# Gated mix of two attentions: first loads in tiles of later work, first maxima by four, projections in two PSUM banks, and a rule by segment for the runs of P @ V

## The chip, the cores and the metric

The kernel runs on one core of one Trainium2 chip. The time is the device time of one execution in microseconds (us). Engines are named as in the profile: PE is TensorE (PEld its weight loads), DVE is VectorE, ACT is ScalarE, POOL is GpSimd, SP is SyncE, which issues most of the DMAs from one queue in the order of the program.

## The reference, cut to what matters

Input x has 2048 tokens of 512 values. Two attentions over x with 32 heads of 16 are mixed by a gate per token.

```python
g = sigmoid((x * gate_w).sum(-1, keepdims=True))
# A: full softmax attention
q, k, v = split(x @ wqkv)                       # 32 heads of 16
a = (softmax(q @ k.T / 4) @ v) @ wo
# B: four segments of 512 tokens, causal inside, with a running memory
for s in range(4):
    p = softmax(qs @ ks.T / 4 + mask)           # within the segment
    a_dot = p @ vs
    a_mem = (phi(qs) @ M) / (phi(qs) @ z + 1e-6)    # phi(t) = t + 1 for t > 0, else exp(t)
    o = sigmoid(beta) * a_mem + (1 - sigmoid(beta)) * a_dot
    M += phi(ks).T @ vs;  z += phi(ks).sum(0)
b = concat(o) @ b_wo
out = g * a + (1 - g) * b
```

## The kernel before, in words

**The head.** The weights and x are split into two parts each (a high part, rounded by ScalarE, and the rest, subtracted by VectorE), and each projection is the sum of three products over four blocks of 128: 12 matmuls of 512 columns into one PSUM bank. Such a group is a *slot* (`slot`, L304). There are 96: for each of four chunks of 512 tokens, four tiles of q, four of k and four of v, first for side A (slots 0 to 47), then for side B (48 to 95, in the order q, v, k). A slot has four *places*, one after each three matmuls; what is posted to a place (`post`, `post_at`) is issued there. So the order on every engine is written out by hand.

After the slot of a q or k tile, `qk_tile` (L343) posts its exit to the next slot: at place 0 ScalarE casts the bank to q1 (L352) and SyncE stores it; at place 1 VectorE subtracts q1 from the bank (q2, L359) and SyncE stores that. For side B, phi needs a minimum (L356), an exponential (L363) and one more VectorE pass (L368), all from the bank. q1 and q2 have two buffers each, the bank pool `pr_ps` three. `mem_k` and `mem_q` do the memory's products.

The weights come through `halves` (L319): two loads of 512 KB into a pool `raws` of three buffers, and four splits posted to slots. The first wq half and the first x chunk take all three buffers; the second wq half (L414), wk and wv follow in the same pool on SyncE's queue.

**Maxima.** Each softmax needs its row maximum before the scores are computed again transposed. `max_part` (L207) does one of 2368 such products (L204) into a bank, and VectorE reduces it (L219). The products of successive parts use different rows of the array. `maxs` gives the order; the maxima run `LEAD` = 96 steps ahead of the scores. The first 96 belong to the head: `some_max` (L514) does two at place 1 and two at place 3 of each slot from slot 72 on (24 after the start of side B), in three banks (`me_sm`).

**The steps.** 2368 steps follow, 74 for each pair of units (a unit is four heads and one segment of 512 queries; 64 steps for A, 10 for B). Each step: one score product (`score_part`, L614) into one of three banks, its exponential on ScalarE (L637), one maximum product into one of four banks. Finished pieces of P @ V wait in `queue`. Every third step (`BURST`) `some_values` (L649) takes up to `MOST` = 3 pieces from it, one more where the queue holds over 6, and one more over 13 (L833); successive pieces of one block of keys form one *run*, a single matmul for each head of up to 512 columns (L670). When a unit of side A after the first segment is done, four bursts go to the output product of an earlier segment instead (`shared`, L747), and pieces of P @ V pile up meanwhile. `first["A", 0, 1]` is step 592, where the second segment of side A begins; the third and fourth begin at 1184 and 1776.

Of the kernel before, what the change touches and what calls it, by code (L numbers as in the profile page):

```python
# [10 lines left out]
F32 = mybir.dt.float32  # L11
# [36 lines left out]
def gated_mix(ctx, tc, x, xT, wqkv, a_wo, b_wq, b_wk, b_wv, b_wo, beta, gate_w, out):  # L48
# [229 lines left out]
    with ExitStack() as p0:  # L278
# [7 lines left out]
        pr_ps = p0.enter_context(tc.tile_pool(name="pr_ps", bufs=3, space=PSUM))  # L286
        me_ps = p0.enter_context(tc.tile_pool(name="me_ps", bufs=2, space=PSUM))
        me_sm = p0.enter_context(tc.tile_pool(name="me_sm", bufs=3, space=PSUM))

        ones = wk1.tile([2, CH], F32, name="ones")  # L290
# [28 lines left out]
        def halves(pool, tag, src, load_slot, split_slot):  # L319

            hold = {}

            def load(i):
                hold["raw", i] = raws.tile([128, 2, D], F32, tag="raw", name="raw")
                nc.sync.dma_start(hold["raw", i], src[256 * i:256 * i + 256].rearrange("(k p) d -> p k d", p=128))

            def split(k):
                if k == 0:
                    hold[0] = pool.tile([128, KT, D], F32R, tag=tag + "h", name=tag + "h")
                    hold[1] = pool.tile([128, KT, D], F32R, tag=tag + "l", name=tag + "l")  # L330
                w = hold["raw", k // 2][:, k % 2]
                nc.scalar.copy(hold[0][:, k], w)
                nc.vector.tensor_sub(hold[1][:, k], w, hold[0][:, k].bitcast(F32))
            post_at(load_slot, 2, lambda: load(0))
            post_at(load_slot, 3, lambda: load(1))
            for k in range(KT):
                post_at(split_slot + k // 2, 2 * (k % 2), lambda k=k: split(k))
            return hold
# [4 lines left out]
        def qk_tile(side, w, xc, o, dst, then=None):  # L343

            ps = pr_ps.tile([128, CH], F32, tag="pr", name="pr")
            slot(ps, lambda a, k: w[a][:, k, o * 128:(o + 1) * 128], lambda b, k: xc[b][:, k, :])
            q1 = wk.tile([128, CH], F32R, tag="q1", name="q1")
            q2 = wk.tile([128, CH], F32R, tag="q2", name="q2")
            ph = {}

            def e0():
                nc.scalar.copy(q1, ps)  # L352
                nc.sync.dma_start(dst[0:16].rearrange("d h t -> (d h) t"), raw(q1))
                if then:
                    ph["mn"] = wk1.tile([128, CH], F32, tag="mn", name="mn")
                    nc.vector.tensor_scalar_min(ph["mn"], ps, 0.0)  # L356

            def e1():
                nc.vector.tensor_sub(q2, ps, q1.bitcast(F32))  # L359
                nc.sync.dma_start(dst[16:32].rearrange("d h t -> (d h) t"), raw(q2))  # L360
                if then:
                    ph["ex"] = wk1.tile([128, CH], F32, tag="ex", name="ex")
                    nc.scalar.activation(ph["ex"], ph["mn"], AF.Exp)  # L363

            def e2():
                if then:
                    ph["ph"] = wk.tile([128, CH], F32, tag="ph", name="ph", bufs=4)
                    nc.vector.scalar_tensor_tensor(ph["ph"], ps, 0.0, ph["ex"], op0=ALU.max, op1=ALU.add)  # L368
                    then(ph["ph"])
            for place, f in enumerate((e0, e1, e2)):  # L370
                post(0, place, f)
# [142 lines left out]
        def some_max(place):  # L514
# [6 lines left out]
            run_todo(m + 1)  # L521
            mnext[0] += 2
            run_late(me_ps, "me", mnext[0])
# [286 lines left out]

    filled = [0]
    n = 0
    while n < nS or queue or beside or filled[0] < len(fill):
# [73 lines left out]
```

## Time and profile before

| | us |
|---|---|
| median of 3 runs (1923.2 to 2658.01) | 1924.52 |
| the profiled execution | 1924.45 |
| its span, first to last instruction | 1922.7 |
| busy: PE / DVE / ACT / POOL | 1878.9 / 1612.1 / 1467.3 / 281.4 |
| first exponential of the steps | about 345 |

The span is the profiled execution without what lies before its first and after its last instruction. A matmul that has been issued and waits in line counts as busy, so TensorE's share is not its load; the other engines' shares are. Stages are read in windows of the same execution.

### The profile page before, as it was taken

Reading aid. Unit: us, or ns where it says so; the run is one execution under the profiler, and the core shown is the slowest. Engines: PE = TensorE matmul, PEld = TensorE weight load, DVE = VectorE, ACT = ScalarE, POOL = GpSimd, SP = SyncE. Lnnn points to the kernel's source line nnn. Section 1 sums busy time; section 2 is a strip of 40 time slices with the busy share of each in tenths; the row PEclk is TensorE's granted clock in tenths of the full one; section 3 lists DMA queues with packets and bytes.
Section 4 is the critical chain, followed back from the end, with each engine's and each line's share of the span. In section 5 each row is a group of like instructions: output and inputs, shape, how many; then the busy total and the mean of one; then the engine's idle time right before and its main releaser. Section 6 shows DMA issues by size and latency. Waiting matters only on the chain.

```text
span 1922.7 us, 46247 instructions
## 1 busy us (share of the span) xinstructions
PE 1878.9 (98%) x18081; PEld 1007.5 (52%) x18081; DVE 1612.1 (84%) x2768; ACT 1467.3 (76%) x2864; POOL 281.4 (15%) x497
## 2 busy tenths in 40 slices
PE   7999999999999999999999999999999999999996
PEld 6888766444444444445445445445444454554554
DVE  4235687899999999999999999999999999999810
ACT  3234332788888888888888888888888888888873
POOL 3000000211111111111112111112111111111210
PEclk9999999899999999999999999999999999999999
DMA  6567645334233324343334343334343334343311
GB/s 206 205 226 259 204 156 167 115 99 129 86 107 92 103 87 110 101 108 102 110 97 111 99 107 102 109 99 111 100 110 100 111 101 113 100 111 99 82 54 41
DMA packets 124362, 227.32 MB, mean 118 GB/s; under 512 B 35144, under 2 KB 50152, under 8 KB 123632
## 3 DMA queue, kind: packets, MB, share of 16 engines
q1 hardware_dynamic: 122560, 223.24, 39.5%
q8 instruction: 144, 2.36, 0.5%
q0 software_dynamic: 1296, 0.59, 0.2%
q14 instruction: 74, 0.61, 0.1%
q10 hardware_dynamic: 288, 0.52, 0.1%
HBM read 155.52 MB, written 67.52 MB: 116 GB/s over the span
## 4 chain that ended last, share of the span: by engine, by line
PE 91%; DMA 3%; ACT 3%; DVE 2%; issue 1%; SPq 0%; ACTq 0%; DVEq 0%
PE ops L670 30%; PE st L614 28%; PE sm L204 13%; PE pr L311 11%; PE ops L747 5%; ACT p L637 2%; PE sm L747 1%; DMA qdA<-q 1%; PE num L468 1%; ACT dg L230 1%; DMA kdB<-q 1%; PE mt_ps L194 1%; DVE pm L219 1%; PE mps L499 0%; DMA qdB<-q 0%
## 5 line engine op out<-in xcount | busy, mean ns | idle before, releaser
L637 ACT ACTIVATE p<-st 128x512 f32<-128x512 f32 x2304 | 1217.6, 606 | 190.6 <-PE sm L204 145.1
L219 DVE TENSOR_REDUCE pm<-sm 128x1 f32<-128x512 f32 x2048 | 1285.6, 681 | 79.0 <-PE sm L204 58.6
L204 PE MATMUL sm<-kA,qA 48*128 48x512 f32 x2048 | 752.0, 448 | 0.3 <-DVE pm L219 0.3
L614 PE MATMUL st<-qA,kA 50*128 50x512 f32 x2048 | 702.8, 440 | 7.2 <-ACT p L637 6.5
L670 PE MATMUL ops<-p,vA 128*17 128x512 f32 (+3 forms) x5784 | 558.9, 473 | 0.0
L614 PEld LDWEIGHTS st<-qA,kA 50*128 50x128 f32 x2048 | 335.4, 186 | 400.6 <-ACT p L637 330.2
L204 PEld LDWEIGHTS sm<-kA,qA 48*128 48x128 f32 x2048 | 338.3, 185 | 26.6 <-DVE pm L219 13.4
L670 PEld LDWEIGHTS ops<-p,vA 128*17 128x17 f32 x5784 | 107.5, 95 | 196.7 <-issue 177.4
L204 PE MATMUL sm<-kB,qB 48*128 48x128 f32 (+2 forms) x896 | 170.6, 294 | 0.0
L204 PEld LDWEIGHTS sm<-kB,qB 48*128 48x128 f32 x896 | 136.4, 189 | 8.4 <-DVE pm L219 0.9
L231 POOL TENSOR_SCALAR_AFFINE_SELECT dg<-dg 128x512 f32<-128x512 f32 x128 | 81.2, 637 | 291.7 <-ACT dg L230 291.7
L614 PE MATMUL st<-qB,kB 50*128 50x384 f32 (+3 forms) x512 | 120.3, 342 | 2.9 <-ACT p L637 2.4
L359 DVE TENSOR_TENSOR q<-pr,q 128x512 fp32r<-128x512 f32 x64 | 43.9, 687 | 89.4 <-ACT q L352 80.2
L187 POOL CAST ms<-nm 128x16 fp32r<-128x16 f32 x64 | 12.6, 197 | 724.9 <-DVE nm L180 496.1
L352 ACT CAST q<-pr 128x512 fp32r<-128x512 f32 x64 | 37.4, 585 | 97.6 <-PE pr L311 64.1
L614 PEld LDWEIGHTS st<-qB,kB 50*128 50x128 f32 x512 | 72.1, 185 | 72.7 <-ACT p L637 60.2
L618 POOL TENSOR_SCALAR_AFFINE_SELECT p<-p 128x512 f32<-128x512 f32 x128 | 78.6, 634 | 92.2 <-ACT p L637 91.5
L240 DVE TENSOR_REDUCE pmB<-sm 128x4 f32<-128x512 f32 x128 | 87.1, 681 | 1.4 <-PE sm L204 1.0
L234 DVE TENSOR_REDUCE pmB<-dg 128x4 f32<-128x512 f32 x128 | 86.6, 677 | 0.4 <-POOL dg L231 0.4
L670 PE MATMUL ops<-p,vB 128*17 128x128 f32 (+3 forms) x1224 | 84.1, 394 | 1.5 <-issue 1.5
L230 ACT COPY dg<-sm 128x512 f32<-128x512 f32 x128 | 76.9, 601 | 1.6 <-PE sm L204 1.0
L721 DVE RECIPROCAL rec<-rec 128x32 f32<-128x32 f32 x44 | 15.1, 342 | 71.5 <-DMA rec<-odA 37.3
(128 smaller groups left out, 1553.3 us busy)
## 6 DMA issues: line engine op xcount, KB each, us to landing
kA<-kdA SPq DMA_DIRECT2D x256, 128.0 KB
vA<-vdA SPq DMA_DIRECT2D x32, 544.0 KB
kA<-kdA SPq DMA_DIRECT2D x256, 64.0 KB
qdA<-q SPq DMA_DIRECT2D x32, 256.0 KB
kdA<-q SPq DMA_DIRECT2D x32, 256.0 KB
qdB<-q SPq DMA_DIRECT2D x32, 256.0 KB
qA<-qdA SPq DMA_DIRECT2D x64, 128.0 KB
kdB<-q SPq DMA_DIRECT2D x32, 256.0 KB
```

Source lines behind the costliest of these rows:

```text
L204: nc.tensor.matmul(ps[:, n0:n0 + n], rows(qt[u][:, :, s * 128:(s + 1) * 128], h, 48), rows(k[:, :, k0:k0 + n], h, 48), start=True, stop=True)
L219: nc.vector.tensor_reduce(pm[:, h, s, kc:kc + 1], ps, axis=AX.X, op=ALU.max)
L230: nc.scalar.copy(dg, blocked(ps))
L231: nc.gpsimd.affine_select(out=dg, in_=dg, pattern=[[0, 4], [-1, 128]], base=0, channel_multiplier=1, compare_op=ALU.is_ge, fill=MASKED)
L234: todo.append((m + MASK_T, lambda: nc.vector.tensor_reduce(to, dg.rearrange("p (h s) t -> p h s t", h=2), axis=AX.X, op=ALU.max)))
L240: nc.vector.tensor_reduce(pm[:, 1, h, 3:7], blocked(ps), axis=AX.X, op=ALU.max)
L311: nc.tensor.matmul(ps, l(a, k), r(b, k), start=(n == 0), stop=(n == 11))
L614: nc.tensor.matmul(ps[:, n0:n0 + CH - q0], rows(k[:, :, b * 128:(b + 1) * 128], h, 50), rows(q[:, :, q0:], h, 50), start=True, stop=True)
L618: nc.gpsimd.affine_select(out=x, in_=x, pattern=[[0, 4], [1, 128]], base=0, channel_multiplier=-1, compare_op=ALU.is_ge, fill=0.0)
L637: nc.scalar.activation(p[:, h], ps, AF.Exp, scale=SCALE)
L670: nc.tensor.matmul(ops[32 * h:32 * h + 17, q0:q0 + 128 * w], v[:, 17 * h:17 * h + 17], p[:, h, c0:c0 + 128 * w], start=(i == 0), stop=done ...
L747: nc.tensor.matmul(ps[32 * t:32 * t + 32, 128 * (j % (ps.shape[1] // 128)):128 * (j % (ps.shape[1] // 128)) + 128], held[side, c][:, o, 12 ...
```

## The change

Five things, in the order of the diff:

- TensorE gets ten 128 x 128 products of the identity ahead of all else.
- `pr_ps` has two banks instead of three, `me_sm` four instead of three.
- `halves` can be given tiles to load into. The second wq half and the first half of wk load into the v tile (`early`, not used before slot 8), the rest of wk and half of wv into the tiles of phi (`pairs`, not used before side B). The loads of wq and wk are issued at the start, those of wv at slot 1.
- `qk_tile`: ScalarE copies the bank to `full` first, and everything else reads `full`; the minimum of phi is GpSimd's.
- `some_max` does four maxima at place 3 only, in the slots 14 to 19, 24 to 31 and 36 on from the start of side B (62 to 67, 72 to 79, 84 to 93). `jam` replaces the rule for how many pieces a burst takes.

```diff
-        pr_ps = p0.enter_context(tc.tile_pool(name="pr_ps", bufs=3, space=PSUM))
+        pr_ps = p0.enter_context(tc.tile_pool(name="pr_ps", bufs=2, space=PSUM))
         me_ps = p0.enter_context(tc.tile_pool(name="me_ps", bufs=2, space=PSUM))
-        me_sm = p0.enter_context(tc.tile_pool(name="me_sm", bufs=3, space=PSUM))
+        me_sm = p0.enter_context(tc.tile_pool(name="me_sm", bufs=4, space=PSUM))
+        idle = me_ps.tile([128, CH], F32, tag="me", name="idle")
+        for _ in range(10):
+            nc.tensor.matmul(idle[:, :128], identf, identf, start=True, stop=True)
...
-        def halves(pool, tag, src, load_slot, split_slot):
+        def halves(pool, tag, src, load_slot, split_slot, tiles=None):
             def load(i):
-                hold["raw", i] = raws.tile([128, 2, D], F32, tag="raw", name="raw")
-                nc.sync.dma_start(hold["raw", i], src[256 * i:256 * i + 256].rearrange("(k p) d -> p k d", p=128))
+                t = tiles[i] if tiles else None
+                if t is None:
+                    t = raws.tile([128, 2, D], F32, tag="raw", name="raw")
+                if isinstance(t, list):
+                    for k in range(2):
+                        nc.sync.dma_start(t[k], src[256 * i + 128 * k:256 * i + 128 * k + 128])
+                        hold["raw", 2 * i + k] = t[k]
+                else:
+                    nc.sync.dma_start(t, src[256 * i:256 * i + 256].rearrange("(k p) d -> p k d", p=128))
...
-            post_at(load_slot, 2, lambda: load(0))
-            post_at(load_slot, 3, lambda: load(1))
+            if load_slot is None:
+                load(0)
+                load(1)
+            else:
+                post_at(load_slot, 2, lambda: load(0))
+                post_at(load_slot, 3, lambda: load(1))
...
+            full = wk.tile([128, CH], F32, tag="full", name="full")
             def e0():
-                nc.scalar.copy(q1, ps)
+                nc.scalar.copy(full, ps)
+                nc.scalar.copy(q1, full)
                 nc.sync.dma_start(dst[0:16].rearrange("d h t -> (d h) t"), raw(q1))
                 if then:
-                    nc.vector.tensor_scalar_min(ph["mn"], ps, 0.0)
+                    nc.gpsimd.tensor_scalar_min(ph["mn"], full, 0.0)
             def e1():
-                nc.vector.tensor_sub(q2, ps, q1.bitcast(F32))
+                nc.vector.tensor_sub(q2, full, q1.bitcast(F32))
...
-                    nc.vector.scalar_tensor_tensor(ph["ph"], ps, 0.0, ph["ex"], op0=ALU.max, op1=ALU.add)
+                    nc.vector.scalar_tensor_tensor(ph["ph"], full, 0.0, ph["ex"], op0=ALU.max, op1=ALU.add)
...
+        early = vp.tile([128, NG, 4, 4, 17], F32, tag="vs", name="vs").rearrange("p g b h e -> p (g b h e)")
+        early = [early[:, 1024 * i:1024 * i + 1024] for i in range(2)]
+        wraw.append(early[0].rearrange("p (k d) -> p k d", k=KT))
+        pairs = [[wk.tile([128, CH], F32, tag="ph", name="ph", bufs=4) for _ in range(2)] for _ in range(2)]
...
+        nc.sync.dma_start(wraw[1], wq_src[:, :, 256:512])
...
-        wraw.append(raws.tile([128, KT, 256], F32, tag="raw", name="raw"))
-        nc.sync.dma_start(wraw[1], wq_src[:, :, 256:512])
-        wAk = halves(wp, "wk", wqkv[:, D:2 * D], 0, 2)
-        wAv = halves(wp, "wv", wqkv[:, 2 * D:3 * D], 0, 4)
+        wAk = halves(wp, "wk", wqkv[:, D:2 * D], None, 2, [early[1].rearrange("p (k d) -> p k d", k=2), pairs[0]])
+        wAv = halves(wp, "wv", wqkv[:, 2 * D:3 * D], 1, 4, [pairs[1], None])
...
-            loads(m + 1 + PRE)
-            for i in range(2):
+            loads(m + 3 + PRE)
+            for i in range(4):
...
-        for n in range(24, 64):
-            for place in (1, 3):
-                posted.setdefault((s0 + n, place), []).append(lambda: some_max(0))
+        for n in range(14, 64):
+            if n // 12 > 2 or n % 12 < 8:
+                post_at(s0 + n, 3, some_max)
...
+    def jam(n):
+        if n < first["A", 0, 1]:
+            return len(queue) > 10
+        return (len(queue) > 6) + (len(queue) > 13 and n >= first["A", 0, last])
...
-                some_values(n, MOST + (len(queue) > 6) + (len(queue) > 13) if n < nS else 8)
+                some_values(n, MOST + jam(n) if n < nS else 8)
```

More of the change, by code (lines that the diff above doesn't have):

```diff
@@ L317, in post_at @@
             posted.setdefault((n, place), []).append(f)
-        def halves(pool, tag, src, load_slot, split_slot):
+        def halves(pool, tag, src, load_slot, split_slot, tiles=None):
             hold = {}
             def load(i):
-                hold["raw", i] = raws.tile([128, 2, D], F32, tag="raw", name="raw")
-                nc.sync.dma_start(hold["raw", i], src[256 * i:256 * i + 256].rearrange("(k p) d -> p k d", p=128))
+                t = tiles[i] if tiles else None
[7 more added lines that the diff above has]
+                    nc.sync.dma_start(t, src[256 * i:256 * i + 256].rearrange("(k p) d -> p k d", p=128))
+                    for k in range(2):
+                        hold["raw", 2 * i + k] = t[:, k]
             def split(k):
@@ L330, in split @@
                     hold[1] = pool.tile([128, KT, D], F32R, tag=tag + "l", name=tag + "l")
-                w = hold["raw", k // 2][:, k % 2]
+                w = hold["raw", k]
                 nc.scalar.copy(hold[0][:, k], w)
                 nc.vector.tensor_sub(hold[1][:, k], w, hold[0][:, k].bitcast(F32))
-            post_at(load_slot, 2, lambda: load(0))
-            post_at(load_slot, 3, lambda: load(1))
+            if load_slot is None:
[4 more added lines that the diff above has]
+                post_at(load_slot, 3, lambda: load(1))
             for k in range(KT):
@@ L511, in mem_k3, with some_max @@
             nc.vector.tensor_scalar_mul(zbd[:, o, 0:8], bmask[:, :, 0], mrun[o][:, 0, 16:17])
-        def some_max(place):
+        def some_max():
             m = mnext[0]
@@ L517, in some_max @@
                 return
-            loads(m + 1 + PRE)
-            for i in range(2):
+            loads(m + 3 + PRE)
+            for i in range(4):
                 max_part(m + i, lambda: me_sm.tile([128, CH], F32, tag="sm", name="sm"))
-            run_todo(m + 1)
-            mnext[0] += 2
+            run_todo(m + 3)
+            mnext[0] += 4
             run_late(me_ps, "me", mnext[0])
```

## The prediction

> **What bounds the kernel now.** I read the page first, then the busy time of each engine by stage, then the stretches of the timeline that stand out. The stages: the head (projections, memory products, first 96 row maxima) lasts until the first exponential at 345 us; then come 2368 steps (a score product, a maximum and a piece of P @ V each), which I cut at steps 592, 1184 and 1776, where the first unit of the next segment of side A begins.
>
> ```profile
> PE 1878.9 (98%) x18081; PEld 1007.5 (52%) x18081; DVE 1612.1 (84%) x2768; ACT 1467.3 (76%) x2864; POOL 281.4 (15%) x497
> ```
>
> TensorE's 98% looks like the bound, but a matmul that waits in line counts as busy. The stages say more (length; then busy time of PE, PEld, DVE, ACT, POOL; granted clock):
>
> ```profile
> 0.00:42.80 42.80, 32.13 (x120) 25.14 (x120) 17.57 (x30) 16.35 (x28) 18.17 (x40) 0.92 0.74 219
> 42.80:146.40 103.60, 103.58 (x457) 85.74 (x458) 28.59 (x43) 33.33 (x60) 1.08 (x4) 1.00 0.61 210
> 146.40:226.30 79.90, 79.16 (x377) 63.16 (x376) 40.52 (x80) 36.23 (x66) 0.66 (x2) 1.00 0.75 252
> 226.30:345.00 118.70, 115.91 (x496) 71.77 (x496) 100.94 (x188) 34.92 (x62) 1.01 (x4) 1.00 0.45 154
> 345.00:727.70 382.70, 376.02 (x2982) 166.80 (x2982) 364.30 (x620) 333.60 (x659) 61.03 (x114) 0.98 0.36 101
> 727.70:1113.10 385.40, 382.70 (x4062) 187.91 (x4064) 369.85 (x632) 336.26 (x663) 65.31 (x112) 1.00 0.39 105
> 1113.10:1499.50 386.40, 382.98 (x4274) 191.80 (x4278) 370.79 (x633) 337.25 (x665) 66.44 (x113) 1.00 0.38 105
> 1499.50:1830.80 331.30, 329.45 (x4044) 171.06 (x4032) 313.04 (x533) 286.13 (x565) 58.14 (x96) 1.00 0.37 103
> ```
>
> In the steps VectorE is busy 364.3 of 382.7, 369.85 of 385.4, 370.79 of 386.4 and 313.04 of 331.3 us. Its reductions set the pace, 0.614 to 0.63 us a step, and all its idle time there is 18.4 + 15.6 + 15.6 + 18.3 = 68 us. TensorE has slack: in the timeline a pair of score and maximum products starts every 0.24 us when nothing holds it, a run of P @ V takes 0.34 us with one piece and 0.99 with four (0.13 fixed, 0.214 a piece), so three steps need 3 x 0.24 + 0.13 + 3 x 0.214 = 1.49 us against the 1.94 they take. In the head it is the other way: from 42.8 to 226 us VectorE is half idle and TensorE works through the projections, 2.72 us for the 12 matmuls of a slot. There a saved TensorE microsecond counts.
>
> Then three places in the head. At 20.7 us TensorE runs dry:
>
> ```profile
> 20.70 0.39 PE L311 MATMUL pr<-xh,wkh 128*128 128x512 f32 x1
> 22.86 0.58 ACT L352 CAST q<-pr 128x512 fp32r<-128x512 f32 x1 [4.51 <-DMA qdA<-q]
> ...
> 23.34 0.62 ACT L332 CAST wkh<-raw 128x512 fp32r<-128x512 f32 x1
> ...
> 24.44 0.68 DVE L333 TENSOR_TENSOR wkl<-raw,wkh 128x512 fp32r<-128x512 f32 x1
> ...
> 25.17 0.79 PE L311 MATMUL pr<-xh,wkl 128*128 128x512 f32 x1 [4.08 <-DVE wkl L333]
> ```
>
> Read upwards: the matmul waits for a weight split, the split stands behind ScalarE's copy L352, and that waits for the store of an earlier q. SyncE's waits tell why the store was late:
>
> ```profile
> SPq L325 <- DVE wkl L333: 7.6, 2, 5.1
> ```
>
> SyncE sat up to 5.1 us at a weight load (L325) that had no free raw buffer, with the stores behind it: q was cast at 12.8 us, its store issued at 17.8.
>
> Second, the maxima between projections:
>
> ```profile
> 263.28 0.40 PE L311 MATMUL pr<-wkh,xh 128*128 128x512 f32 x1
> 263.61 0.49 PE L204 MATMUL sm<-kA,qA 48*128 48x512 f32 x2
> 264.03 0.50 PE L311 MATMUL pr<-wkh,xl 128*128 128x512 f32 x1
> 264.37 0.39 PE L311 MATMUL pr<-wkl,xh 128*128 128x512 f32 x1
> ```
>
> A plain slot takes 2.72 us, one with two such pairs 4.04: 0.66 a pair, though two maxima run side by side (the two are one entry of 0.49). Most of it is the change from projection to maxima and back: 0.33 + 0.42 + 0.34 us between the four starts where 0.23 is usual between projections.
>
> Third, the end of the head:
>
> ```profile
> 341.22 0.51 PE L204 MATMUL sm<-kA,qA 48*128 48x512 f32 x2
> 344.27 0.38 PE L546 MATMUL gps<-identf,glog 128*16 128x128 f32 x1 [2.54 <-DVE jk L430]
> ```
>
> TensorE waits 2.54 us for VectorE, which is behind with maxima, gate products and subtractions.
>
> **The change, part by part.**
>
> Warm-up: ten 128 x 128 f32 products on the identity are 20 records. The identity is ready at 1.4 us, the first projection starts at 5.98. In the cold stretch at 345.6 us four 128-column records together take 0.94 us, 0.24 each, so they fill about 4.7 us, just to the first projection. What they buy is small: the first slot runs 5.98 to 10.72, but its last input split (L404) ends at 9.41 and the next slot's weights at 10.27 (L404 at 9.58). So 0.4 us.
>
> Early loads: the wq half and the wk rows go to tiles with no other use yet, wv is issued a slot later with one raw buffer that is free by 10.3 us. SyncE no longer blocks; it issues 4 loads earlier at 0.4 us each, all behind the loads of x that slot 0 needs. Slots 4, 5, 7, 9 and 10 took 7.73, 4.41, 2.83, 3.51 and 2.89 us; at 2.72 that is 5.0 + 1.7 + 0.1 + 0.8 + 0.2 = 7.8 us. Slot 5 was slow because after the 4.47 us without a matmul the clock was granted at half for 6.8 us. If wk lands late I lose up to 3 of this.
>
> Two projection banks: ScalarE now copies every q and k tile to SBUF (64 copies, 0.59 us each by L352) before it casts. In a plain slot this makes 0.59 + 0.62 of 2.72 us; with splits (two of 0.62) 2.45, still inside. The bank is free after the first copy instead of after VectorE's subtraction, so two banks wait about as long as three did: a late cast of tile n then held slot n+3, and now delays the copy of tile n+1, which also holds slot n+3. I take 0 here; the stall at slot 52 (0.9 us) stays. Bounds 0 to +6.
>
> The minimum of phi goes from VectorE (24 x 0.69 = 16.5 us) to GpSimd. No GpSimd minimum is in the trace; the nearest rows are its select (0.64 us, L618) and its multiplication of two tiles (1.28, L733). I take 1.0. It works while ScalarE casts (0.62), so the exponential waits some 0.4 us, and ScalarE (1.2 + 0.4 + 0.63 + 0.59 in slots of 4.5) has room. Now VectorE's subtraction and phi read two SBUF tensors while GpSimd reads SBUF; no row shows these side by side. If they excluded each other, 24 x 1.28 = 31 us of VectorE waiting would be the most. The page "SBUF — State Buffer" of the Trainium skill (Who interferes with whom) states such a rule: an exclusive lock, for the whole instruction, between a VectorE instruction with two SBUF inputs and a GpSimd instruction that reads SBUF. By it the head would gain little; the third case below prices it.
>
> Maxima by four: 24 groups in 24 slots instead of 48 in 24. A second pair behind the first costs the 0.24 of a pair in the steps, so 0.66 + 0.24 = 0.90 a group instead of 1.32: 24 x 0.42 = 10.1 us. Between 0 (a second pair as dear as the first) and that. They begin in slot 62 instead of 72 and leave out the slots where k and the memory sums load VectorE until slot 84: slots 72 and 84 took 0.45 and 0.8 us more than their TensorE work. Slot by slot from 62: +5.4 (six groups, 62 to 67), -3.3 (72 to 79), -5.5 (80 to 83), -4.5 (84 to 93), and -4.0 at the end (94 and 95 took 11.4 us to the first exponential; 2 x 2.72 and 2 for the gate and the table load remain). Sum -11.9. VectorE's cover: a q slot has 2.5 for four maxima and 1.4 for q and phi against 4.5 us of TensorE, a v slot up to 5.3 against 4.5, so I allow +3.
>
> The first steps: from 344.2 us the clock was at half for 10.2 us, after that gap of 2.54, and the first 148 steps took 0.662 us each where the next took 0.633, 4 us. With the gap at 1 to 2 us I count half, -1.5. The page "TensorE: Matmul & The Clock Gate" of the Trainium skill (Part 1) puts the cold state behind an idle window of about 3.4 us; this trace shows it after 2.54, so the row decides, and by the page the gap would never have been enough.
>
> P @ V by segment: I replayed the loop's counting for both rules, pieces and runs alone. Runs: segment 0 from 195 to 293, segment 1 from 215 to 176, segment 2 from 228 to 173, the last unchanged at 238; 876 in all against 880. So it moves runs, it doesn't save them: +98 x 0.13 = 13 us of TensorE in segment 0, -94 x 0.13 = -12 in the next two, all in TensorE's slack of 0.45 us per three steps. What can move is VectorE's 49.6 us of idle time in these segments. VectorE has four banks, 2.5 us of work, against blocks of at most 1.33 (1 + 4 pieces) before and 0.99 after. Ranked by burst in the trace, VectorE idles 0.09 to 0.13 us after a run of four, 0.07 after three, 0.02 after 3 + 1: by that the new mix gives +8 us in segments 1 and 2 and 0 in segment 0; by smaller blocks alone up to -12. I take -3, since the shorter block is the one thing that all rows agree on.
>
> Sum: -0.4 - 7.8 + 0 - 11.9 - 1.5 - 3 = -24.6. The profiled execution took 1924.45 us with a span of 1922.7; the median of the runs shown is 1924.52, so 1924.5 - 24.6 = 1900 us, 1.3% less. A measurement of this kernel tells about 2% from no change, here 38 us.
>
> **The rivals.** (1) Forecast: the head gains some 21 us, the steps stay, 1886 to 1914; chance 0.66. (2) The steps gain too: if half of VectorE's idle time in segments 0 to 2 goes (25 us) and all of the cold start, 1924.5 - 20.1 - 4 - 25 = 1875. For: the idle time follows TensorE's blocks. Against: the number of runs is the same. 0.17. (3) The head's gain is eaten: VectorE and GpSimd exclude each other around the minima. All 31 us would give 1931, half of them 1915; TensorE's longer slots hide a part, so 1918. Against: no phi in side A, and VectorE has room outside v slots. 0.11. (4) Slower: ScalarE is now the only one that frees a bank, and its cast waits for a q buffer whose store must land. Landings in the chain were 5.41, 8.35, 6.17, 7.04, 8.40 and 2.72 us; two buffers with 8.4 + 0.62 + 0.3 turn at 4.66 us a tile against 2.72. It decides from a landing of 4.5 us plus the slack of one bank, 7.2 us, tile after tile; 24 such tiles cost 24 x 1.94 = 46.6, 1946 us. Against: before had the same two buffers, and only slots 4, 9 and 52 stalled. 0.06, half of it beyond 2%.
>
> **How the numbers follow.** Faster by over 2% is case 2: 0.17. Slower by over 2% is half of case 4: 0.03. The rest, 0.80, lies within. The range takes case 1, the near side of 2 and case 3: 1880 to 1922.
>
> **What would show it.** Right: no TensorE gap over 1 us before 40 us, slot 12 starting near 40.2 instead of 48.4; slots with four maxima near 3.6 us; the first exponential near 325 instead of 345; the steps still at 0.645 to 0.655 us; VectorE at 95 to 97% there. Wrong: GpSimd's minimum ending VectorE's waits, ScalarE's copy ending TensorE's, or steps that differ by over 0.01 us.

## The result and the profile after

The changed kernel takes **1908.24 us** (median of 4 executions, 1904.02 to 1909.87) against 1925.66 for the kernel before (4 executions beside it): a ratio of 0.991 with a 95% interval from 0.9887 to 0.9934. One execution of before, at 2658.01 us, was disturbed and is left out of that ratio. The profiled execution took 1908.66 us with a span of 1906.9, so 15.8 us less span than before. The forecast was 1900 us, in a range from 1880 to 1922, a change of less than 2%.

The page's line of engines, to be set beside that of before:

```profile
PE 1875.4 (98%) x18133; PEld 1014.6 (53%) x18133; DVE 1597.1 (84%) x2744; ACT 1508.1 (79%) x2928; POOL 319.1 (17%) x521
```

VectorE lost the 24 minima (2768 to 2744 instructions), GpSimd gained them, and ScalarE has 64 copies more. The shares hardly moved. The same by stage, cut where before was cut (start:end and length; busy time of PE, PEld, DVE, ACT, POOL; granted clock, DMA share, GB/s):

```profile
0.00:42.80 42.80, 37.51 (x147) 29.11 (x148) 19.55 (x32) 22.40 (x39) 18.25 (x40) 0.96 0.75 231
...
144.80:226.30 81.50, 78.84 (x358) 59.50 (x357) 45.66 (x83) 41.68 (x74) 14.02 (x11) 0.98 0.70 225
226.30:338.80 112.50, 109.05 (x521) 76.15 (x519) 84.03 (x163) 50.71 (x86) 24.95 (x21) 1.00 0.53 182
338.80:720.00 381.20, 379.83 (x3763) 194.03 (x3767) 363.47 (x619) 334.63 (x661) 61.23 (x114) 0.97 0.36 100
720.00:1102.70 382.70, 380.69 (x3763) 177.65 (x3766) 369.16 (x634) 336.34 (x664) 65.50 (x112) 1.00 0.41 106
1102.70:1486.10 383.40, 380.71 (x3838) 178.25 (x3832) 369.62 (x633) 337.27 (x665) 67.28 (x114) 1.00 0.40 105
```

The three windows of the first segments are 381.2, 382.7 and 383.4 us long, where they were 382.7, 385.4 and 386.4. VectorE's idle time in them (length less busy) is 17.7, 13.5 and 13.8 instead of 18.4, 15.6 and 15.6. The head ends at 338.8, not at 325.

The rest of this document uses one table. It is made from the starts of the instructions in each trace: slot n starts with the 12n-th projection product, "first exp" is the first exponential of the steps, and the steps are counted by their exponentials.

| us | slot 12 | slot 48 | slot 62 | slot 95 | first exp | steps 0-148 | 148-592 | 592-1184 | 1184-1776 | 1776-2272 | rest |
|---|---|---|---|---|---|---|---|---|---|---|---|
| before | 48.4 | 146.4 | 191.0 | 337.6 | 346.3 | 97.2 | 284.7 | 385.4 | 387.0 | 330.7 | 91.5 |
| after | 46.9 | 144.8 | 193.3 | 331.8 | 338.8 | 100.0 | 281.1 | 382.7 | 383.4 | 330.9 | 89.9 |
| small_late | 42.9 | 143.0 | 191.7 | 330.2 | 337.2 | 100.0 | 281.1 | 382.7 | 383.4 | 330.7 | 88.9 |
| jam_undone | 47.5 | 145.4 | 193.8 | 332.4 | 339.4 | 100.8 | 282.9 | 385.2 | 387.0 | 330.6 | 90.8 |
| combined | 42.8 | 141.4 | 185.6 | 324.0 | 328.1 | 103.0 | 281.2 | 382.7 | 383.4 | 330.9 | 89.7 |

So the 15.8 us are 7.4 from the head, 6.8 from the steps and 1.6 from the rest. The prediction had 20 from the head and 4.5 from the steps. Two questions follow: where did 13 us of the head's forecast gain go, and why did the steps gain more?

**The head, first stall.** Slot 4 takes 2.72 us now, where it took 7.73. But slots 5, 7 and 8 take 3.91, 5.52 and 4.45 (before: 4.41, 2.83, 2.72). Lines of the timeline of after (start, length, engine, line, operation, in brackets the idle time before it and what ended it):

```profile
23.48 0.62 ACT L371 CAST q<-full 128x512 fp32r<-128x512 f32 x1 [3.23 <-DMA qdA<-q]
23.50 1.93 POOL L449 DMA_DIRECT2D bt<-beta  x3 [1.17 <-DMA kB<-ones]
24.12 0.32 SPq L372 DMA_DIRECT2D qdA<-q  x1
...
33.02 0.62 ACT L371 CAST q<-full 128x512 fp32r<-128x512 f32 x1 [4.41 <-DMA qdA<-q]
...
34.17 0.50 PE L315 MATMUL pr<-wvh,xl 128*128 128x512 f32 x1 [2.50 <-ACT full L370]
```

Read upwards: TensorE waits 2.50 us for the copy that frees a bank (L370). The copy stands on ScalarE behind the cast of another tile (L371), and that cast waited 4.41 us for a buffer whose store had to land. That store was issued at 24.12 and landed at about 33, nearly 9 us later. SyncE was not blocked in between. The same stretch in the DMA queues (24 to 32 us; packets, MB, share of 16 engines):

```profile
q0 software_dynamic: 216, 0.03, 27.7%
q1 hardware_dynamic: 283, 0.50, 16.5%
```

GpSimd's queue (q0) moved 0.03 MB and took more of the engines' time than SyncE's (q1) with 0.50. Most of these bytes are in six packets of 4096 bytes, but most of the time is not: 50 packets of 64 bytes, between 27.0 and 32.0 us, took 0.65 us each, 32 of the queue's 35 us of engine time. By their order these are the last four loads of beta (L449, 512 bytes each in 4-byte elements).

**The head, second stall.** At slots 52 and 53, which take 5.05 and 4.45 us (before: 3.43 and 2.88), again from the timeline of after:

```profile
144.12 6.55 SPq L336 DMA_DIRECT2D raw<-b_wk  x2
...
151.23 0.57 SPq L372 DMA_DIRECT2D qdB<-q  x1
...
158.53 0.62 ACT L371 CAST q<-full 128x512 fp32r<-128x512 f32 x1 [4.79 <-DMA qdB<-q]
159.05 1.13 ACT L345 CAST wvh<-raw 128x512 fp32r<-128x512 f32 x2
...
160.09 0.58 ACT L370 COPY full<-pr 128x512 f32<-128x512 f32 x1
...
160.72 0.52 PE L315 MATMUL pr<-wkh,xl 128*128 128x512 f32 x1 [2.17 <-ACT full L370]
```

SyncE stands 6.55 us at the two loads of b_wk, which need free raw buffers; the stores of v and q wait behind them. What SyncE waits for there is VectorE's split of the weights loaded before (b_wv), by the list of its waits in after (us in total, times, longest):

```profile
SPq L336 <- DVE wkl L346: 5.7, 1, 5.7
```

That split is posted to slot 49, so the whole stall moves with the projections. The same place in before:

```profile
145.69 5.89 SPq L325 DMA_DIRECT2D raw<-b_wk  x2
...
159.28 0.59 ACT L352 CAST q<-pr 128x512 fp32r<-128x512 f32 x1 [5.67 <-DMA qdB<-q]
...
160.66 0.50 PE L311 MATMUL pr<-wkh,xl 128*128 128x512 f32 x1 [0.55 <-DVE q L359]
```

The product that ends the wait starts at 160.66 us in before and at 160.72 in after, but that is chance. Five kernels with b_wk loaded at slot 47 (the last three are edits of after, described below):

| us | before | after | small_late | loads_undone | min_on_vector |
|---|---|---|---|---|---|
| slot 48 starts | 146.4 | 144.8 | 143.0 | 147.2 | 147.6 |
| slot 52 takes | 3.43 | 5.05 | 5.18 | 5.06 | 4.97 |
| slot 53 takes | 2.88 | 4.45 | 4.45 | 2.85 | 2.86 |

In all nine kernels with the changed exit and this place for the loads, slot 52 takes 4.9 to 5.2 us, whether TensorE comes early or late. So nothing that was won earlier is given back here; the stall itself has grown. From the start of slot 48 to the end of the wait there are 15.93 us in after and 14.31 in before, 1.62 more. Half of that, 0.81, lies ahead of the late cast (158.53 in after, 159.28 in before): ScalarE's copy puts the first cast of q 0.62 later, and with it the split that SyncE waits for. The other half lies behind it: in before 1.38 us pass from that cast to the product, in after 2.19, since the copy that frees the bank stands on ScalarE behind the cast and two weight casts. Slot 53 is longer only where the clock went to half (see the last section).

**The end of the head.** The time from slot 95 to the first exponential fell from 8.65 to 7.05 us. Timeline of after:

```profile
335.32 0.62 ACT L371 CAST q<-full 128x512 fp32r<-128x512 f32 x1
...
335.96 1.28 ACT L572 ACT_TABLE_LOAD   x1
...
337.54 1.28 ACT L661 ACT_TABLE_LOAD   x1
...
338.83 1.57 ACT L661 ACTIVATE p<-st 128x512 f32<-128x512 f32 x3
...
339.48 0.79 PE L638 MATMUL st<-qA,kA 50*128 50x512 f32 x1 [3.04 <-ACT p L661]
```

ScalarE comes late from its cast, loads the table for the gate's sigmoid, and then the one for the exponential. TensorE waits for that, 3.04 us, instead of for VectorE (2.54 before). From 338.6 us the clock is granted at half for 23.9 us (before: 10.2).

### The profile page after: what moved, and what is told of

Same layout as the page of the kernel before. It is cut to its first block, busy times and chain, and to the rows that moved or that the text cites. A ratio compares the mean times of both kernels' runs of the same rounds, so it can differ in the third digit from the quotient of the medians.

```text
span 1906.9 us, 46497 instructions
## 1 busy us (share of the span) xinstructions
PE 1875.4 (98%) x18133; PEld 1014.6 (53%) x18133; DVE 1597.1 (84%) x2744; ACT 1508.1 (79%) x2928; POOL 319.1 (17%) x521
## 4 chain that ended last, share of the span: by engine, by line
PE 92%; ACT 3%; DMA 2%; DVE 1%; issue 1%; POOL 1%; SPq 0%; ACTq 0%; POOLq 0%; DVEq 0%
PE ops L694 31%; PE st L638 28%; PE sm L204 14%; PE pr L315 11%; PE ops L771 6%; ACT p L661 1%; PE sm L771 1%; DMA qdA<-q 1%; POOL mn L375 1%; PE mt_ps L194 1%; PE num L491 1%; ACT dg L230 0%; DMA vs<-wqkv 0%; DMA qdB<-q 0%; PE mps L522 0%
## 5 line engine op out<-in xcount | busy, mean ns | idle before, releaser
L204 PE MATMUL sm<-kA,qA 48*128 48x512 f32 x2048 | 742.9, 447 | 0.0
L204 PEld LDWEIGHTS sm<-kA,qA 48*128 48x128 f32 x2048 | 334.1, 185 | 20.8 <-issue 6.5
L378 DVE TENSOR_TENSOR q<-full,q 128x512 fp32r<-128x512 f32 x64 | 44.1, 689 | 97.8 <-ACT q L371 87.2
L187 POOL CAST ms<-nm 128x16 fp32r<-128x16 f32 x64 | 12.7, 198 | 650.6 <-DVE nm L180 416.2
L370 ACT COPY full<-pr 128x512 f32<-128x512 f32 x64 | 37.3, 584 | 54.2 <-PE pr L315 54.1
L745 DVE RECIPROCAL rec<-rec 128x32 f32<-128x32 f32 x44 | 15.1, 344 | 70.9 <-DMA rec<-odA 36.7
```

Source lines behind the costliest of these rows:

```text
L204: nc.tensor.matmul(ps[:, n0:n0 + n], rows(qt[u][:, :, s * 128:(s + 1) * 128], h, 48), rows(k[:, :, k0:k0 + n], h, 48), start=True, stop=True)
```

## The experiments

Each kernel is the changed one with the edit shown; the last two put several edits together. small_late, jam_undone, combined and combined_filled have four executions beside those of the kernel before; the others have one profiled execution, and are compared by their stages.

**small_late.** GpSimd's loads of gate_w and beta are posted to slot 20 instead of the start.

```diff
-        nc.gpsimd.dma_start(gw, gate_w...)
-        for o in range(NO): nc.gpsimd.dma_start(bt[:, o:o + 1], beta...)     # and bt4
+        def load_small(): ...                                               # the same nine loads
+        post_at(20, 0, load_small)
```

> The kernel after, with GpSimd's small loads (gate_w and the eight 4-byte-element loads of beta) issued at slot 20 instead of at the start. Theory S (GpSimd's slow packets hold up SyncE's stores, which hold q buffers): the stalls of slots 5, 7 and 8 go, slot 12 starts near 40.5 us instead of 46.9, the first exponential near 333 instead of 339, and the total falls by 4 to 7 us. Theory V (the volume of the weight loads ahead of the stores sets the landing): slot 12 still starts at 46 to 47 us and the total is unchanged.

Measured: 1905.83 us (ratio 0.9893, 0.9877 to 0.991). Slots 7 and 8 are back at 2.72 and slot 12 starts at 42.9 instead of 46.9. The place of the small loads at the start was the cause, as the kernels below bear out. But slots 18 to 21, beside the place where they now stand, take 2.3 us more (slot 20 alone 4.43), so slot 48 starts only 1.7 earlier than in after, and slot 62 too. The total is 2.4 us under after's median, which is inside the spread of after's own four executions.

**loads_undone** and **loads_undone_small_late.** The early loads go back to the raw pool, without and with the edit above.

```diff
-        wAk = halves(..., None, 2, [early[1]..., pairs[0]])
-        wAv = halves(..., 1, 4, [pairs[1], None])
+        wAk = halves(..., 0, 2)
+        wAv = halves(..., 0, 4)          # and the second wq half into raws, after split_wq(1)
```

> The kernel after, with the weight loads as before (in the three raw buffers, SyncE waiting for them), small loads at the start. Theory S: the early loads hardly matter, because the same slow stretch of the store queue lies at 24 to 33 us either way; slot 12 starts at 46.5 to 49 us against 46.9 after and 48.4 before. Theory V or the prediction's own (SyncE blocked at a load is what costs): slot 4 stalls again by 4 us or more and slot 12 starts at 50 us or later.

> Both at once: weight loads as before, small loads at slot 20. With the slow stretch out of the way this shows what the early loads are worth by themselves. The prediction's step (blocked SyncE, 5 us at slot 4 and its cold clock) gives slot 12 at 45 us or later against 40.5 with early loads; theory S alone gives slot 12 at 41 to 43 us.

Measured: slot 12 at 49.2 and 45.5 us, totals 1909.48 and 1908.75; slot 4 takes 6.73 and 6.53 again. With after (46.9) and small_late (42.9) this is a square: the early loads are worth 2.4 and 2.6 us at slot 12, the late small loads 3.8 and 4.0. These are single profiles, and with after's early code unchanged slot 12 lay between 45.8 and 50.9 in seven of them. The worth of the late small loads stands clear of that: with the early loads in place, slot 12 lies at 41.4 to 42.9 in all three kernels that post them late. The worth of the early loads does not: they take the stall out of slot 4 wherever the exit is the changed one, but what is left of that at slot 12 rests on one profile in each row.

**jam_undone.** The rule of before for the pieces of a burst.

```diff
-                some_values(n, MOST + jam(n) if n < nS else 8)
+                some_values(n, MOST + (len(queue) > 6) + (len(queue) > 13) if n < nS else 8)
```

> The kernel after with the rule of before for the pieces of a burst. If the rule is what shortened the steps (theory R: VectorE starves less behind shorter blocks of TensorE), steps 592 to 1776 take 772 us again instead of 766, steps 148 to 592 about 284.5 instead of 281, and the total is 6 to 10 us above the kernel after. If the steps gained from something in the head (theory H: another phase between the engines, other banks), they stay at 766 and 281 and the total is unchanged.

Measured: 1917.41 us (ratio 0.9949, 0.9931 to 0.9967, against 0.991 with the new rule, some 8 us). The stages say the same: +1.8 us in the steps 148 to 592, +2.4 and +3.6 in the next segments, 7.8 in all. Windows of jam_undone for these two segments:

```profile
723.10:1108.30 385.20, 382.55 (x4078) 188.09 (x4082) 370.11 (x633) 336.27 (x665) 65.49 (x112) 1.00 0.40 105
1108.30:1495.30 387.00, 383.60 (x4280) 192.15 (x4269) 371.25 (x634) 337.31 (x666) 67.16 (x114) 1.00 0.38 105
```

VectorE idles 15.1 and 15.8 us in them, against 13.5 and 13.8, and the same reductions keep it busy 0.9 and 1.6 us longer. So over half of what the rule is worth there is idle time; the rest is busy time, for which the trace gives no reason.

**exit_direct.** Everything reads the bank again, which has two buffers now; the minimum is VectorE's.

```diff
-                nc.scalar.copy(full, ps)
-                nc.scalar.copy(q1, full)
+                nc.scalar.copy(q1, ps)          # and ps for full in the minimum, q2 and phi
```

> The kernel after without ScalarE's copy: q1, the minimum (VectorE again), q2 and phi read the bank as before, still with two projection banks. The prediction's step (the copy is what makes two banks do for three): TensorE waits for VectorE's subtraction and phi, the slots of side B cost 1 to 3 us more each with phi, the first exponential comes 10 to 40 us later than 338.8. Rival: the copy buys nothing, because banks are free in time either way; within 3 us of 338.8.

Measured: 1919.93 us, the first exponential at 349.5 instead of 338.8. Slots 58, 59, 70, 71, 82 and 83 take 5.2 to 5.3 us instead of 4.0 to 4.2. Of these 10.7 us, 1.5 lie before slot 12, where executions of one code differ by more; the rest comes from slots 12 to 62 (4.3 us) and 62 to 95 (5.4), less 0.5 at the end. The edit moves the minimum to the bank as well. In the six slots TensorE waits 0.6 to 0.9 us at a time for VectorE's phi, the last reader of the bank; in after no product of these slots waits for a bank. The copy is what lets two banks do for three there.

**maxima_by_two.** Pairs at two places from slot 72 on, as before.

```diff
-        for n in range(14, 64):
-            if n // 12 > 2 or n % 12 < 8:
-                post_at(s0 + n, 3, some_max)
+        for n in range(24, 64):
+            for place in (1, 3):
+                post_at(s0 + n, place, some_max)        # two in some_max instead of four
```

> The kernel after with the maxima at the places of before (two at place 1 and two at place 3, from slot 72), in four banks. The prediction's step (0.42 us a group for changing between projections and maxima, and stalls on VectorE): slots 62 to 95 take 146 to 148 us instead of 138.5, a plain slot with maxima 4.04 instead of 3.61. Rival (a fourth bank is what helped): 138 to 141 us.

Measured: 144.8 us from slot 62 to slot 95, against 138.5 (and 146.6 in before); a plain slot with maxima takes 4.04 against 3.61. In after such a slot reads, in the timeline:

```profile
265.80 0.40 PE L315 MATMUL pr<-wkh,xh 128*128 128x512 f32 x1
266.13 0.74 PE L204 MATMUL sm<-kA,qA 48*128 48x512 f32 x4
...
266.80 0.50 PE L315 MATMUL pr<-wkh,xl 128*128 128x512 f32 x1
```

From projection to projection 1.00 us with four maxima in it, 0.23 without: 0.77 at this place, and 0.89 over the whole slot. The total of maxima_by_two is 1910.99 us, only 2.3 above after, since its first 148 steps took 96.4 us instead of 100.0; more on that below.

**min_on_vector.** The minimum of phi goes to VectorE, but reads `full`.

```diff
-                    nc.gpsimd.tensor_scalar_min(ph["mn"], full, 0.0)
+                    nc.vector.tensor_scalar_min(ph["mn"], full, 0.0)
```

> The kernel after with phi's minimum on VectorE again (0.69 us there against 1.5 on GpSimd, 24 times). Theory G (VectorE has room in these slots and GpSimd's 1.5 us only lengthens the chain to phi): slots 60, 72 and 84 lose 0.3 to 0.7 us each, slots 62 to 95 take 135 to 138 us instead of 138.5. Prediction's step (VectorE is short there, 16.5 us taken from it): slots 62 to 95 take 140 to 146 us.

Measured: 1904.56 us in a single execution; slots 60, 72 and 84 take 4.15, 5.01 and 5.01 us instead of 4.80, 5.51 and 5.51, and from slot 60 to slot 95 it is 1.9 us shorter. One instruction by its line (min/median/max of its duration in ns), first in after, then in this kernel:

```profile
L375 POOL TENSOR_SCALAR mn<-full x24: 1486/1488/2030, 174.2 to 304.1; 128x512 f32<-128x512 f32 x24
```

```profile
L375 DVE TENSOR_SCALAR mn<-full x24: 417/420/437, 175.3 to 305.4; 128x512 f32<-128x512 f32 x24
```

VectorE does it in 0.42 us from `full`, in before it took 0.685 from the bank, and GpSimd takes 1.49. The Trainium skill, page "VectorE: DVE Perf Modes", section "What auto-detection actually checks", states that a single source and a destination both in SBUF let VectorE use a faster mode; this pair of numbers agrees.

**b_wk_late.** The loads of b_wk three slots later.

```diff
-                wBk = halves(wp, "wv", b_wk, s0 + 11, s0 + 15)
+                wBk = halves(wp, "wv", b_wk, s0 + 14, s0 + 16)
```

> The kernel after with the load of side B's k weights posted to slot 50 instead of 47 and its splits to slots 52 and 53. Theory B (SyncE stands at that load until a raw buffer is free, the v store and the q stores behind it): slots 52 and 53 take 2.7 to 3 us each instead of 5.05 and 4.45, slot 62 starts near 189.5 instead of 193.3. Rival V (1 MB of v and the q stores simply take their 7 us to land): slots 52 and 53 lose less than 1 us together.

Measured: slots 52 and 53 take 2.72 each, and slots 48 to 62 take 44.4 us instead of 48.5. The place of these loads is shown to be the cause of that stall. How they act is not told apart: in after SyncE issues the first store of q 2.3 us after its cast has ended and it lands 7.2 us later; here it is issued at once, has none of the b_wk loads ahead of it, and lands within 4.8 us. The total, 1908.54, is no shorter, because slots 7 to 9 took 4.00, 6.73 and 5.28 in this execution.

**gate_by_exp** and **gate_early.** The first computes the sigmoid of the gate with the exponential's table; the second does that too, and finishes the gate in slot 94, with the last logits a slot earlier.

```diff
-        nc.scalar.activation(gt[:16, 0], gps[:16, :128], AF.Sigmoid)
+        nc.scalar.activation(gt[:16, 0], gps[:16, :128], AF.Exp, scale=-1.0)
+        nc.vector.tensor_scalar(gt[:16, 0], gt[:16, 0], 1.0, 1.0, op0=ALU.mult, op1=ALU.add)
+        nc.vector.reciprocal(gt[:16, 0], gt[:16, 0])
```

> The kernel after with the gate's sigmoid as 1 / (1 + exp(-t)): ScalarE's table for the exponential stays loaded at the end of the head. Theory C (the two table loads, 1.28 us each, are on the path to the first exponential, and TensorE's 3.04 us gap behind them brings the 23.9 us at half clock): the first exponential comes 2 to 2.6 us earlier (336.2 to 336.8), the half clock is gone or shorter than 10 us, the first 148 steps take 94 to 97 us instead of 100, total 5 to 8 us less. Rival D (the first steps are slow because TensorE works in short runs there, whatever the gap): 2.5 us earlier, but still 99 to 101 us for 148 steps and a half clock of 20 us.

> The kernel after with the gate finished inside the head: the last gate products one slot and its load two slots earlier, the transposition and the gate (by the exponential) at slot 94. Nothing but the projections stands then before the first steps. Theory C (idle TensorE and VectorE at the end of the head bring the half clock): the first exponential near 331 to 332.5 instead of 338.8, no TensorE gap over 1 us there, the half clock gone or under 10 us, the first 148 steps 94 to 97 us instead of 100; total 10 to 14 us less than after. Theory D (the first steps bring it by themselves): 6 to 7 us earlier, still a half clock of 20 us or more and 100 us.

Measured: slot 95 to the first exponential takes 4.23 and 4.06 us instead of 7.05; the two table loads were on the path, 2.8 us. Totals 1905.07 and 1902.40. But the half clock stayed, 20.5 us of it in the first and 13.7 in the second, where no gap of TensorE ahead of it is over 1 us. A single long gap of TensorE is not needed for it.

**combined.** small_late (with one load of beta, spread by two small products, posted to slot 23), b_wk_late and gate_early together.

> The kernel after with three changes: the gate finished at slot 94; b_wk loaded at slot 50; beta loaded once as 32 values at slot 23 and spread by two small products on TensorE, gate_w at the same place, so that GpSimd's slow small packets no longer run beside the first stores. By the single runs: 4 us at slots 7 and 8, 4 us at slots 52 and 53, 6.5 us at the end of the head and, if theory C holds, 4 to 6 us of half clock: 1890 to 1895 us. If what is won early is given back at the next late store or landing, as with the small loads alone: 1896 to 1900 us.

Measured: 1900.98 us (ratio 0.987, 0.9849 to 0.9891), ahead of both kernels by its median, though its interval just touches after's. The gains of the head add up: the first exponential comes at 328.1, 10.7 us before after's. But the first 148 steps take 103.0 us, 3 more than in after. The clock is at half for 23.9 us, as it was there, and the first run of P @ V now waits 2.62 us for its load of v, which is issued 1.2 us after the first exponential instead of 1.8 before it.

**combined_filled.** combined, with the minimum on VectorE, the gate's eight loads at step 30, and extra work for TensorE before P @ V begins.

```diff
+        if 3 <= n < 8:
+            for h in range(4):
+                nc.tensor.matmul(ops[32 * h:32 * h + 17, 0:128], identf[:, 0:17], identf, ...)
```

> The kernel combined with three edits. The minimum of phi is VectorE's (worth 1.9 us when that edit was made alone). The eight small loads of the gate values on GpSimd's queue, issued in combined just before the first step, are issued at step 30. In the steps 3 to 7, whose products of P @ V do not exist yet, TensorE does four extra products of the identity a step (17 by 128 each), which add work and change no output. Theory D (the clock is halved because TensorE has too little to do in the first steps, before P @ V begins): the half-clock stretch, 23.9 us in combined, goes or shrinks to at most one window of 3.4 us, the steps 0 to 148 take 94 to 96 us instead of 103, and the total comes to 1888 to 1893 us. Rival E (the clock is lowered by something the head leaves behind, whatever the first steps do): the stretch stays at 10 us or more, the steps 0 to 148 take 98 us or more, and the total is 1895 to 1900. For the loads of the gate: the first run of P @ V waits under 1 us for vA instead of 2.62 if they slow that load, and the same 2.6 us if only SyncE's own queue sets when it lands. First exponential near 326 (combined 328.1).

Measured: 1899.49 us (1893.85 to 1900.52; ratio 0.9854, 0.9805 to 0.9904), the profiled execution 1893.85. Windows of it around the first steps (first exponential at 325.3):

```profile
326.00:330.00 4.00, 3.68 (x43) 1.84 (x43) 2.99 (x7) 3.57 (x8) 0.91 (x2) 0.87 0.68 227
330.00:334.00 4.00, 4.00 (x31) 1.53 (x23) 1.30 (x2) 2.08 (x4) 0.84 (x2) 0.50 1.01 236
```

The clock falls to half at 329.0, while the extra products run, and stays there for 13.7 us. Steps 0 to 148 take 99.7. The idea that TensorE has too little to do in the first steps falls, at least in this form. The first run of P @ V shows no wait for v any more, but it also starts later after the first exponential, so what slowed that load is not told apart. Its lead of 1.5 us over combined's median is inside the spread of both.

## Why the prediction was right, and which terms were not

The total lies inside the range and in the likeliest case, 8 us above its value. Part of that is luck, since terms that were wrong cancelled. By its steps:

**Warm-up, -0.4.** Slot 0 starts 0.3 us earlier and takes 4.99 us instead of 4.74. There is no gain to be seen. It was not tried by itself.

**Early loads, -7.8: the term that failed.** The step "SyncE no longer blocks" was right, slot 4 lost its stall. One reading under it was off: the longest wait in the row of SyncE's waits, 5.1 us, is not at this place but at the loads of b_wk near 146 us, where the second stall begins. The early wait in that row is 2.5 us, one of several behind the 8.3 us that the four loads took on SyncE (9.4 to 17.8 us). The wait of 5.1 stayed, and is 5.7 in after. What failed is the conclusion that the slots behind it would then run at 2.72. Slots 0 to 11 took 41.2 us instead of 42.5, a difference inside the spread of the seven profiles named above. The next thing late was the stores of q, slowed by the small loads on GpSimd's queue; the prediction looked at what SyncE's queue was blocked by, and not at what shared the DMA engines with it. Its fourth case had the landings of the chain, up to 8.40 us, but asked for late ones tile after tile; here a few tiles were enough to take back most of this term.

**Two banks and the copy, 0, "the stall at slot 52 stays (0.9 us)".** The copy's worth is shown in the main (exit_direct), and plain slots kept their 2.72. The stall at 52 did not stay at its size: slots 48 to 62 took 3.9 us more than before, inside the bounds that went to +6. Of that, 1.6 is the longer wait, 1.6 the half clock in slot 53 and 0.7 mostly slot 60, which waits for the minimum (4.15 with VectorE's). The missed step is the copy's place: the prediction set the copy of the next tile against VectorE's subtraction and found them about equal, and left out that on ScalarE the copy delays the cast ahead of the late store and stands behind two weight casts after it. The sign that was named as wrong, "ScalarE's copy ending TensorE's" waits, did appear, in both stalls: behind a late store the cast holds ScalarE, and the copy for the next tile stands behind it.

**GpSimd's minimum, 1.0 us with bounds 0.64 to 1.28.** It takes 1.49, outside the bounds. The lines nearest to it were a select and a two-tile product, and neither bounded it. It made the exponential wait 8.5 us in all (VectorE's minimum in before: 5.1) and cost 1.9 us between slots 60 and 95. The dearer point is that the change had a better place at hand: from `full`, VectorE needs 0.42. The case in which VectorE and GpSimd exclude each other was hardly seen: nine of VectorE's subtractions overlapped a minimum on GpSimd, and took 0.67 to 0.69 us, as all of them do. Eight of these minima took 1.49 to 1.51 us; the ninth, which started together with the subtraction, took 2.03. That is 0.5 us once, against the 31 that the prediction had as the most.

**Maxima by four, -11.9.** The mechanism was right, slot for slot: 62 to 67 +5.1 (+5.4 predicted), 72 to 79 -2.8 (-3.3), 80 to 83 -5.2 (-5.5), 84 to 93 -3.8 (-4.5), a slot at 3.61 (3.6). The last term, 94 to the first exponential, gave -2.8 of -4.0. Its base was misread: the first exponential of before starts at 346.3 us, not at 345, so slots 94 and 95 took 12.7 us and not 11.4. And I allowed 2 us for the gate and the table, where there were two table loads of 1.28 behind a busy ScalarE; 9.9 us remained. In all -9.8.

**First steps, -1.5.** They took 2.8 us more. The reason given, a shorter gap, was wrong twice: the gap grew to 3.04, and with no gap over 1 us ahead of it (gate_early) the half clock is still there.

**P @ V by segment, -3 with bounds -12 and +8.** The sign was right, and the term too small: jam_undone is 7.8 us slower in the steps 148 to 1776. The reason (smaller blocks leave VectorE less idle) accounts for 1.6 of 2.4 and 2.0 of 3.6 us in the two segments that were measured. The ranking of idle time by the burst, which gave +8, did not carry over: counted burst by burst in the steps 592 to 1776, VectorE idles 0.08 us with one run of four in after, and 0.12 to 0.15 in before. Another 1.8 us of the steps 148 to 592 is gone in jam_undone too (282.9 against 284.7), so the rule did not bring them; their cause is open.

Of the signs named beforehand, those of the steps came out: 0.651 us a step from the first exponential to step 2272, VectorE at 95 to 96%, slots with four maxima at 3.61. Those of the head did not: slot 12 at 46.9 instead of 40.2, and the first exponential at 338.8 instead of 325. Of the rivals, the one in which the steps gain as well came true in small, 6.8 us of its 29, and the one of late landings held for the two stalls alone.

So the head fell short by 12.7 us, 10.6 of them before slot 62, and the first steps by 4.3; the later steps gained 6.6 more than their term, and 1.6 came from the end, for which there was no term. The total came nearer than its terms.

## What to carry to other kernels

Where a saved stretch of a stage ends at a wait, look for the *next* wait before booking the gain, and then ask what ends that one. A queue that stands at a load for a free buffer holds every store behind it. Here the buffer was freed by the kernel's own later work, so the stall came along with the work, as long as ever, and the copy that was added to that chain made it longer; moving the load was what removed it. List all queues that share the DMA engines with a store that something waits for, small element-wise loads above all. And when a tile has been copied to SBUF, ask again which engine does the passes over it; the answer may differ from the one for PSUM.

## What was not expected of the hardware

**Small loads.** Between 24 and 32 us, 216 packets of 0.03 MB together took 27.7% of 16 DMA engines' time, nearly all of it in 50 packets of 64 bytes, and a store of 256 KB issued at 24.12 us took nearly 9 us to land.

**The clock.** Half-clock stretches came in multiples of 3.41 us, but for those that the end of the kernel cuts: 3.4 in after at 34.8 and 161.1, behind TensorE gaps of 2.50 and 2.17, and 10.2 to 27.3 at the start of the steps. The single ones cost 1.73 us each: slots 8 and 53 took 4.45 instead of 2.72, with no wait of their own beyond the one in front. But such a gap does not always bring one. Nine kernels have the stall of slot 52 with a TensorE gap of 1.97 to 2.30 us; the half clock follows in four of them (gaps of 2.08 to 2.30) and not in the other five (1.97 to 2.25). The page "TensorE: Matmul & The Clock Gate" of the Trainium skill (Part 1) has a window of 3413 ns, which agrees with the multiples; its idle window of about that length ahead of the half clock is not what these gaps show.

**The stretch in the first steps.** In the profiles of these kernels it lasts 10.2 to 27.3 us, and steps 0 to 148 take 96.4 to 103.0 us, 3 to 9 more than 148 steps at the 0.633 of the next 444. The two go together only roughly: with 13.7 us of half clock these steps took 96.4 and 96.5 us in two kernels and 99.5 and 99.7 in two others. The totals go with the mean granted clock of an execution: of combined_filled's four, the one with a mean granted clock of 0.995 took 1893.85 us and the three with 0.991 took 1899.1 to 1900.5; of combined's, 1897.03 at 0.995 and 1900.7 to 1904.3 at 0.990 to 0.992. It came with a TensorE gap (after, 23.9 us), without one (gate_early, 13.7) and with extra products in the first steps (combined_filled, 13.7). What sets its length stays open.
